# Score groups and late products with v on one ring of two PSUM tiles, block products on two bank pairs, and a new list of work

## The chip, the cores and the metric

The kernel runs on one core of one Trainium2 chip. The metric is device time in microseconds (us), from the start of the program to its end. TensorE (PE in the profile) multiplies matrices into PSUM, which has eight banks of 128 x 512 fp32 values; VectorE (DVE), ScalarE (ACT) and GpSimd (POOL) do the rest, and SyncE (SP) starts the transfers. PE's weight loads are listed apart, as PEld.

## What is computed

Attention with a mask by blocks of 64 rows, and behind it a two-layer feed-forward block with a squared ReLU. Batch 8, 8 heads, 576 rows, head size 64; 512 features, 2048 hidden.

```python
def _attn_ref(q, k, v):
    block = 64
    scale = 1.0 / np.sqrt(D)
    scores = scale * np.matmul(q, k.transpose(0, 1, 3, 2))
    mask = block_i >= block_j
    scores = np.where(mask, scores, -1000000000.0)
    scores = scores - np.max(scores, axis=-1, keepdims=True)
    attn = np.exp(scores)
    attn = attn / (np.sum(attn, axis=-1, keepdims=True) + 1e-09)
    return np.matmul(attn, v).astype(np.float32)
...
def _moe_ref(x, w_in, w_out):
    h = x @ w_in
    r = np.maximum(h, 0.0)
    g = r * r
    return (g @ w_out).astype(np.float32)
```

## The kernel before

**Tiling.** A pass is one pair of heads of one batch element. Passes 0 to 7 do the first three blocks of rows of batch elements 0 and 1, passes 8 to 15 the other six, and passes 16 to 39 all nine blocks of elements 2 to 7. A pass from 8 on has three score groups (`A20_0`, `A20_1`, `A20_2` in pass 20): PE writes the scores of two to four blocks of rows into one PSUM tile `side` of two banks, DVE takes each block's negative maximum (`B`, tile `nmx`), ACT the exponentials (`C`, tile `p`, sums `sm`), POOL and DVE the inverse of the sum (`S`, `R`), and ACT and DVE write the scaled rows as two fp16 parts (`H` and `L`, tile `p_rows`). A transfer turns them (`T`, `p_turned`), PE multiplies them with v (`G`, PSUM tile `px`), and `X` moves the result to SBUF.

**Chunks.** Twelve chunks of 384 tokens go through the feed-forward block, in the order 0, 1, 2, 4, 3, 5, 7, 6, 8, 10, 9, 11. The first three are plain: `ph` is one product with the first weights for 128 hidden features, `pos`, `sqr`, `top`, `rem` make its square into two fp16 parts (`hidden`). From chunk 4 on the first layer is a seven-product block scheme: for each of four groups of a chunk, PE runs p1, p2, p6, p5, p7, p4, p3 (`p14_0` is p1 of chunk 4, group 0). p1, p6, p7 and p4 add up in one bank, X; p2, then p5 and p3, use another, B. Between them ACT or DVE copies X (`c11` after p1, `c12` after p6, `c22` after p7, `c21` after p4) and DVE adds B to those copies (`a11` after p2, `a22` after p5, `a12` after p3). A product may start when the copy of what it overwrites or adds to is done. The scheme needs weights that are combined once on DVE, POOL and ACT (`t0_0` to `t3_17`; `p14_0` needs `t0_17`, the last of group 0's). `po` is the second layer: 16 steps of three products for each of three blocks of tokens, with the result scaled (`ob`) and stored (`out`).

**Order.** `ORDER` is a list of all pieces of work by name, with the engine where there is a choice (`:D`, `:A`, `:P` for DVE, ACT, POOL). `Plan.run` makes them in that order, and `Lines` ties each instruction to the one before it on its engine. So every engine works through its own part of the list, in order, and an instruction that waits holds up all that stands behind it on that engine. The list alone sets the order; the costs and ranks in `plan_all` are not used by it. How pieces of different engines stand to each other in the list says nothing of time.

**PSUM.** Banks are taken in turn from rings, and a piece that takes one waits until the pieces that read its last content are done. Up to pass 13 there are two `side` tiles, two `pair` banks (transposes, `ph`, `po`) and two banks `x` (transposes, `px`, sums for the norm, weight maxima). From pass 14 (`ALONE`) on all score groups use `side0` alone. The three banks thus given up (`side1` has two, `pair1` one) become a ring `group` of three for the block products, and `pair0` serves `po`. Two functions carry this: `side_of`, and `bank_of`, which closes the early pool:

```python
        if t["i"] >= ALONE:
            return 0
...
            homes[ring] = [ps_g.tile([P, 512], F32, name=f"group{n}") for n in range(3)]
```

## Time and profile before

| | |
|---|---|
| median of three runs | 963.83 us (962.95 to 963.94) |
| profiled execution | 963.4 us, of which the span is 961.6 us |
| PE busy, PE weight loads | 936.5 us, 602.6 us |
| DVE, ACT, POOL busy | 764.7, 638.6, 267.9 us |
| mean granted clock of PE | 0.995 of 2.4 GHz |
| by line of the chain that ended last | PE 81%, DVE 10%, ACT 3% |

The span is the profiled stretch of the execution; the other 1.8 us lie around it. A busy PE is a PE whose matmuls overlap without a gap in the records; the ends of matmuls are modelled, so a short wait can lie inside busy time. All instructions have line 331, since a helper records them: they are told apart by the names of their tiles.

### The profile page before, as it was taken

What the parts mean: (1) busy time and instruction counts of PE and PEld (TensorE: products, weight loads), DVE (VectorE), ACT (ScalarE), POOL (GpSimd) and SP (SyncE); (2) the same over time, 40 slices, a digit from 0 to 9 for tenths busy, and PEclk for the clock granted to TensorE, in tenths of its full rate; (3) what the DMA queues carried; (4) which work ended last, traced back from release to release, by engine and by line L of the source; (5) the groups of instructions that cost most, each with busy time, mean ns of one, the idle gap of its engine ahead of it and who ended that gap; (6) DMA issues with size and microseconds to landing.
All of it is one profiled execution on the core that took longest, in us unless ns stands there. A gap on an engine that the chain in (4) does not pass through costs nothing.

```text
span 961.6 us, 21188 instructions
## 1 busy us (share of the span) xinstructions
PE 936.5 (97%) x8145; PEld 602.6 (63%) x8145; DVE 764.7 (80%) x1703; ACT 638.6 (66%) x1585; POOL 267.9 (28%) x371
## 2 busy tenths in 40 slices
PE   8899899999998999999999999999999999999998
PEld 5455444545554784785676675686675675596675
DVE  6999997789899997899879788698879777656331
ACT  6999986765895786885475576678657555365330
POOL 4586401222255541224032032031112012011110
PEclk9999999999999999999999999999999999999999
DMA  9915477656855318435665346564473354400001
GB/s 358 399 63 186 153 163 164 139 135 136 188 115 121 83 51 190 104 63 118 124 155 123 78 107 112 119 150 94 86 176 84 74 117 81 91 13 12 12 1 45
DMA packets 221650, 114.93 MB, mean 120 GB/s; under 512 B 195290, under 2 KB 203756, under 8 KB 221548
## 3 DMA queue, kind: packets, MB, share of 16 engines
q1 hardware_dynamic: 221548, 113.57, 48.5%
q8 instruction: 64, 1.05, 0.4%
q14 instruction: 38, 0.31, 0.1%
HBM read 58.21 MB, written 9.46 MB: 70 GB/s over the span
## 4 chain that ended last, share of the span: by engine, by line
PE 81%; DVE 10%; ACT 3%; POOL 2%; issue 2%; DMA 2%; SPq 0%; DVEq 0%; ACTq 0%; POOLq 0%
PE pair L331 40%; PE group L331 24%; PE side L331 8%; PE px L331 6%; DVE nmx L331 2%; DVE p_rows L331 2%; PE po L331 2%; DVE w L331 2%; DMA w<-in_w_in 1%; POOL w L331 1%; DVE xt_all L331 1%; DVE stw L331 1%; DMA vraw<-in_v 1%; ACT p L331 1%; DVE x L331 1%
## 5 line engine op out<-in xcount | busy, mean ns | idle before, releaser
L331 PE MATMUL pair<-w,hidden 128*128 128x512 f16 (+1 forms) x1680 | 382.1, 376 | 1.0 <-DVE ob L331 0.9
L331 PEld LDWEIGHTS <-hidden 128*128 128x128 f16 x1776 | 168.5, 98 | 179.0 <-issue 11.7
L331 PEld LDWEIGHTS <-w 128*128 128x128 f16 x2304 | 200.4, 98 | 56.9 <-issue 10.3
L331 ACT ACTIVATE p<-side,nmx 128x576 f32<-128x576 f32 (+8 forms) x264 | 140.1, 541 | 94.3 <-DVE nmx L331 45.6
L331 POOL TENSOR_TENSOR hidden<-r,hidden 128x384 f16<-128x384 f32 x103 | 104.0, 1020 | 219.7 <-ACT hidden L331 204.6
L331 PE MATMUL group<-xt_all,w 128*128 128x192 f16 x1728 | 161.8, 247 | 0.8 <-DVE xt_all L331 0.5
L331 DVE SCALAR_TENSOR_TENSOR p_rows<-p,rs,p_rows 128x64 f16<-128x64 f32 (+7 forms) x264 | 147.2, 578 | 11.0 <-ACT p_rows L331 8.8
L331 DVE TENSOR_REDUCE nmx<-side 128x1 f32<-128x192 f32 (+8 forms) x288 | 123.4, 481 | 27.2 <-PE side L331 26.4
L331 POOL TENSOR_SCALAR sm<-sm 128x2 f32<-128x2 f32 (+2 forms) x104 | 34.5, 332 | 333.2 <-ACT p L331 316.0
L331 PE MATMUL group<-xt_all,turned_w 128*128 128x192 f16 x1296 | 122.8, 246 | 0.0
L331 PEld LDWEIGHTS <-turned_w 128*128 128x128 f16 x1296 | 108.1, 98 | 14.2 <-issue 4.9
L331 ACT ACTIVATE p_rows<-p,rs 128x64 f16<-128x64 f32 (+11 forms) x173 | 90.3, 554 | 31.8 <-DVE rs L331 21.2
L331 ACT ACTIVATE r<-group,rescale 128x384 f32<-128x384 f32 x111 | 63.7, 579 | 69.2 <-PE group L331 61.5
L331 ACT ACTIVATE r<-r 128x384 f32<-128x384 f32 x177 | 90.9, 523 | 20.0 <-DVE r L331 17.7
L331 ACT CAST hidden<-r 128x384 f16<-128x384 f32 x172 | 84.7, 507 | 28.8 <-DVE r L331 19.1
L331 DVE SCALAR_TENSOR_TENSOR r<-group,rescale,r 128x384 f32<-128x384 f32 x108 | 65.9, 613 | 45.8 <-PE group L331 32.5
L331 PE MATMUL side<-qk 64*64 64x512 f32 (+2 forms) x480 | 97.0, 498 | 3.5 <-ACT p L331 3.4
L331 PE MATMUL pair<-xt_all,w 128*128 128x384 f16 x576 | 98.9, 326 | 1.1 <-DVE xt_all L331 0.7
L331 PE MATMUL side<-ks,qk 64*64 64x192 f32 (+4 forms) x576 | 91.9, 424 | 0.0
L331 PE MATMUL px<-p_turned,v 128*64 128x384 f16 (+5 forms) x1168 | 66.8, 269 | 0.3 <-ACT p_turned L331 0.3
L331 PEld LDWEIGHTS <-v 128*64 128x64 f16 x1128 | 48.5, 110 | 21.5 <-issue 11.3
L331 DVE TENSOR_TENSOR hidden<-r,hidden 128x384 f16<-128x384 f32 x89 | 51.3, 579 | 7.5 <-ACT hidden L331 7.1
(154 smaller groups left out, 1060.3 us busy)
## 6 DMA issues: line engine op xcount, KB each, us to landing
qk<-in_qk SPq DMA_DIRECT2D x32, 576.0 KB
ks<-in_ks SPq DMA_DIRECT2D x32, 320.0 KB
vraw<-in_vm SPq DMA_DIRECT2D x30, 256.0 KB
w<-in_w_out SPq DMA_DIRECT2D x10, 512.0 KB
out<-ob SPq DMA_DIRECT2D x17, 256.0 KB
w<-in_w_in SPq DMA_DIRECT2D x8, 512.0 KB
out<-ob SPq DMA_DIRECT2D x26, 128.0 KB
hidden<-in_w_in SPq DMA_DIRECT2D x6, 512.0 KB
```

The lines of the kernel that those rows point to most:

```text
L331: i = make(*a, **k)
```

## The change

All eight banks are given out once, for the whole program: two `side` tiles of two banks, two banks `pair`, two banks `single`.

- Score groups take the two `side` tiles in turn to the end (ring `s`). The products with v of passes 12 to 39 take one tile of the same ring, one half for each of the two parts.
- X of group g is `pair0` for even g and `pair1` for odd g, and B is the other one. So p1 of a group goes into the bank that p3 of the group before has filled, and waits for that group's `a12`; p2 waits for that group's `c21`.
- `single` serves as ring `x` early on; later `single0` is ring `y` (norm sums, v's maxima, two of the last four outputs) and `single1` is `po`.
- `ORDER` is another list. The rest of the code, the sizes and the number of matmuls stay.

```diff
-p0 A0 B0 C0 p1 A1 A2 B1 S0 R0 C1 r0 max0_0 prelu0_0 B2 D0:P S1 R1 C2 r1 prelu0_1 bits0_0 A3 p2 D1:P E0 F0:A A4 r2 B3 C3 E1 max0_1 A5 bits0_1 S2
+p0 p1 r0 r1 p2 A0 r2 r3 A1 r4 B0 C0 p3 B1 r5 C1 S0 A2 R0 r6 D0:D r7 prelu0_0 max0_0 bits0_0 A3 r8 B2 r9 S1 E0 prelu0_1 bits0_1 keys8 R1 max0_1 C2
...
-    ps_x = ctx.enter_context(tc.tile_pool(name="ps_x", bufs=2, space=PSUM))
-    sides = [ps_b.tile([P, 1024], F32, name="side0")]
-    pairs = [ps_b.tile([P, 512], F32, name="pair0")]
-    early = ExitStack()
-    ps_e = early.enter_context(tc.tile_pool(name="ps_e", bufs=1, space=PSUM))
-    sides.append(ps_e.tile([P, 1024], F32, name="side1"))
-    pairs.append(ps_e.tile([P, 512], F32, name="pair1"))
-    homes = {"mm": pairs, "po": pairs[:1]}
-    turns_of = dict(mm=0, po=0, g=0)
+    bank = lambda name, n: ps_b.tile([P, 512 * n], F32, name=name)
+    pairs, singles = ([bank(f"{name}{n}", 1) for n in range(2)] for name in ("pair", "single"))
+    homes = {"s": [bank(f"side{n}", 2) for n in range(2)], "mm": pairs, "x": singles, "y": singles[:1], "po": singles[1:]}
+    turns_of = {ring: 0 for ring in homes}
...
-        if ring not in homes:
-            early.close()
-            ps_g = ctx.enter_context(tc.tile_pool(name="ps_g", bufs=1, space=PSUM))
-            homes[ring] = [ps_g.tile([P, 512], F32, name=f"group{n}") for n in range(3)]
...
-            ps = box["ps"] = sides[side_of(t, group)]
+            ps = box["ps"] = bank_of("s")
...
-        full = ps_x.tile([P, 512], F32, tag="x", name=f"px_{u}_{g}")
+        if t["whole"]:
+            full = bank_of("x")
+        else:
+            if "home" not in t:
+                t["home"] = bank_of("s")
+            full = t["home"][:, 512 * (1 - g) :]
...
-            box[name] = bank_of("g")[:, :CH]
+            box[name] = pairs[(g + (name == "B")) % 2][:, :CH]
...
-                    ("p1", lows("01") + weights + ([f"p2{ck}_{g - 1}"] if g else []), ("g",)),
-                    ("p2", [f"p1{k}"], ("g",)),
+                    ("p1", lows("01") + weights + ([f"p2{ck}_{g - 1}"] if g else []), (f"g{g % 2}",)),
+                    ("p2", [f"p1{k}"], (f"g{1 - g % 2}",)),
```

Two places in the order, with the numbers of the tiles. The first is DVE's part around the first product of the block scheme, `p14_0`. `nmx_3_1_0_8` holds the maxima of `A21_2` and `nmx_3_2_0_4` those of `A22_0`; `t0`, `t2`, `t3` are combined weights; the row `w1<-t0` is `t0_17`. Before:

```order
L331 SCALAR_TENSOR_TENSOR p_rows_93<-p32_3_1_0_7_3604,rs_3_1_0_7_3718,p_rows_93 128x128
L331 TENSOR_SCALAR m_3_2_0_3734<-pm_3_2_0_3646 128x2
L331 TENSOR_TENSOR turned_w_105<-t2_AluOpType.subtract_0_3639,turned_w_105 128x2x256
L331 SCALAR_TENSOR_TENSOR p_rows_93<-p32_3_1_0_7_3604,rs_3_1_0_7_3718,p_rows_93 128x384
L331 SCALAR_TENSOR_TENSOR p_rows_93<-p32_3_1_0_7_3604,rs_3_1_0_7_3718,p_rows_93 128x512
L331 TENSOR_REDUCE nmx_3_1_0_8_3748<-side0_75 128x1 x2
L331 TENSOR_SCALAR nmx_3_1_0_8_3748<-nmx_3_1_0_8_3748 128x2
L331 TENSOR_TENSOR xt_all_106<-x32_97,xt_all_106 128x768
L331 TENSOR_TENSOR w1_107<-t0_AluOpType.subtract_1_3752,w1_107 128x2x256
L331 TENSOR_TENSOR xt_all_106<-s2_2_1_3721,xt_all_106 128x384
L331 TENSOR_REDUCE nmx_3_2_0_4_3883<-side0_75 128x1 x4
```

After:

```order
L331 TENSOR_TENSOR w1_103<-t0_AluOpType.subtract_1_3526,w1_103 128x2x256
L331 TENSOR_TENSOR s2_2_1_3563<-s1_2_1_3552,x32_93 128x384
L331 TENSOR_TENSOR xt_all_102<-s1_2_1_3552,xt_all_102 128x384
L331 TENSOR_TENSOR t3_AluOpType.subtract_0_3618<-w1_103 128x512
L331 SCALAR_TENSOR_TENSOR p_rows_89<-p32_3_0_0_8_3528,rs_3_0_0_8_3543,p_rows_89 128x576
L331 TENSOR_TENSOR t3_AluOpType.subtract_0_3618<-t3_AluOpType.subtract_0_3618,w1_103 128x512 x2
L331 TENSOR_TENSOR xt_all_102<-s2_2_1_3563,xt_all_102 128x384
L331 SCALAR_TENSOR_TENSOR p_rows_89<-p32_3_0_0_8_3528,rs_3_0_0_8_3543,p_rows_89 128x448
L331 TENSOR_TENSOR turned_w_101<-t3_AluOpType.subtract_0_3618,turned_w_101 128x2x256
L331 TENSOR_REDUCE nmx_3_2_0_4_3674<-side0_76 128x1 x4
L331 TENSOR_SCALAR nmx_3_2_0_4_3674<-nmx_3_2_0_4_3674 128x4
L331 TENSOR_REDUCE nmx_3_1_0_8_3687<-side1_77 128x1 x2
```

Before, `A21_2` and `A22_0` both stand in `side0`; now they stand in `side1` and `side0`, and the two maxima follow each other. `t0_17` stood behind the maxima of `A21_2` and stands ahead of them now. Up to and with it DVE's part of the list has 629 instructions before and 601 now. PE's part up to `p14_0` has 396 matmuls of `po` before and 336 now, and `G20`'s 42 matmuls no longer stand there; the rest is the same work but for two small matmuls of v's maxima.

The second place is ACT's part in chunk 3, the second chunk of the block scheme, from the first copies of group 0 to those of group 1 (`r12_3_1` is the copy `c12` of chunk 3, group 1). Before:

```order
L331 ACTIVATE r12_3_0_5005<-group2_3839,rescale_112 128x384
L331 ACTIVATE p32_4_0_0_8_5008,sm_4_0_0_8_5009<-side0_75,nmx_4_0_0_8_4956 128x576
L331 ACTIVATE p32_4_0_0_8_5008,sm_4_0_0_8_5009<-side0_75,nmx_4_0_0_8_4956 128x448
L331 CAST xt_all_106<-x32_97 128x2x96
L331 ACTIVATE r11_3_1_5026<-group1_3838,rescale_112 128x384
L331 ACTIVATE r22_3_0_5058<-group2_3839,rescale_112 128x384
L331 ACTIVATE p_rows_93<-p32_4_1_0_4_4903,rs_4_1_0_4_4954 128x128
L331 ACTIVATE p_rows_93<-p32_4_1_0_4_4903,rs_4_1_0_4_4954 128x64
L331 CAST hidden_109<-r11_3_0_4989 128x2x192
L331 ACTIVATE r12_3_1_5095<-group1_3838,rescale_112 128x384
L331 ACTIVATE r21_3_0_5097<-group2_3839,rescale_112 128x384
```

After:

```order
L331 ACTIVATE ob_4_2_5059<-single1_75,uv_4_4519 128x512
L331 ACTIVATE ob_4_2_5059<-ob_4_2_5059,uv_4_4519 128x512
L331 ACTIVATE r21_3_0_5089<-pair0_72,rescale_108 128x384
L331 ACTIVATE r12_3_0_4994<-r12_3_0_4994 128x384 x2
L331 CAST hidden_105<-r12_3_0_4994 128x2x192
L331 ACTIVATE r21_3_0_5089<-r21_3_0_5089 128x384
L331 CAST hidden_105<-r22_3_0_5029 128x2x192
L331 ACTIVATE r12_3_1_5141<-pair1_73,rescale_108 128x384
L331 CAST hidden_105<-r21_3_0_5089 128x2x192
```

Before, copies of group 1 (bank `group1`) stand between those of group 0 (`group2`): two groups are open at once. Now the last copy of group 0, `r21_3_0`, stands ahead of group 1's `r12_3_1`. Over the nine chunks p1 of the next group stands ahead of the last product of a group 25 times of 27 before, and once now.

## Rows read from the trace of the kernel before

**Rows 1.** the page: span and part 1 (busy us, share, instructions).

```profile
span 961.6 us, 21188 instructions
...
PE 936.5 (97%) x8145; PEld 602.6 (63%) x8145; DVE 764.7 (80%) x1703; ACT 638.6 (66%) x1585; POOL 267.9 (28%) x371
```

**Rows 2.** busy time by stretch: us, PE, PEld, DVE, ACT, POOL, clock, DMA.

```profile
0.00:120.00 120.00, 103.82 (x799) 61.47 (x800) 108.75 (x256) 108.56 (x289) 70.79 (x104) 0.97 0.63 232
120.00:300.00 180.00, 180.00 (x1315) 92.90 (x1314) 157.58 (x359) 130.76 (x327) 48.10 (x67) 1.00 0.66 147
300.00:322.00 22.00, 18.88 (x171) 12.28 (x173) 19.26 (x32) 11.83 (x28) 11.94 (x12) 0.92 0.45 82
322.00:820.00 498.00, 496.85 (x4740) 338.44 (x4733) 416.78 (x943) 333.03 (x834) 117.03 (x168) 1.00 0.50 110
820.00:830.00 10.00, 9.10 (x48) 4.08 (x43) 6.36 (x15) 3.40 (x8) 0.19 (x1) 1.00 1.00 202
830.00:955.00 125.00, 125.00 (x1064) 91.16 (x1063) 55.42 (x102) 50.98 (x100) 19.90 (x21) 1.00 0.05 13
955.00:961.60 6.60, 2.85 (x27) 2.32 (x24) 0.54 (x1) 0.00 (x0) 0.00 (x0) 0.98 0.30 79
```

**Rows 3.** timeline of PE, 303 to 314: start, length, work [idle, releaser].

```profile
304.09 2.26 PE L331 MATMUL px<-p_turned,v 128*64 128x192 f16 x42
306.40 2.10 PE L331 MATMUL pair<-w,hidden 128*128 128x512 f16 x9
311.58 0.49 PE L331 MATMUL side<-qk 64*64 64x320 f32 x2 [3.07 <-ACT p L331]
...
313.52 3.44 PE L331 MATMUL group<-xt_all,w 128*128 128x192 f16 x24
```

**Rows 4.** timeline of DVE and ACT in the same stretch.

```profile
305.50 3.08 DVE L331 SCALAR_TENSOR_TENSOR p_rows<-p,rs,p_rows 128x384 f16<-128x384 f32 x2
...
308.50 1.27 DVE L331 TENSOR_REDUCE nmx<-side 128x1 f32<-128x576 f32 x2
...
310.08 0.74 ACT L331 ACTIVATE p<-side,nmx 128x576 f32<-128x576 f32 x1 [2.97 <-DVE nmx L331]
...
312.06 0.69 DVE L331 TENSOR_TENSOR w<-_AluOpType.subtract,w 128x512 f16<-128x512 f32 x1 [1.22 <-ACT w L331]
```

**Rows 5.** busy time and granted clock just after 312, and around 826.

```profile
312.00:315.00 3.00, 3.00 (x29) 2.04 (x20) 2.94 (x6) 1.17 (x3) 2.84 (x3) 0.63 0.54 100
315.00:318.00 3.00, 3.00 (x30) 2.83 (x28) 2.97 (x7) 2.10 (x8) 1.35 (x2) 0.80 0.00 0
824.00:827.00 3.00, 2.10 (x11) 0.87 (x10) 2.02 (x4) 0.37 (x2) 0.00 (x0) 1.00 1.12 204
```

**Rows 6.** waits of PE: who for whom, us in total, times, longest.

```profile
PE pair L331 <- DVE ob L331: 0.9, 1, 0.9
...
PE group L331 <- DVE xt_all L331: 0.5, 1, 0.5
...
PE group L331 <- DVE r L331: 0.2, 1, 0.2
```

**Rows 7.** timeline of PE and ACT, 393 to 398: one group's first products.

```profile
393.80 2.14 PE L331 MATMUL group<-xt_all,w 128*128 128x192 f16 x24
...
394.99 0.58 ACT L331 ACTIVATE r<-group,rescale 128x384 f32<-128x384 f32 x1 [1.87 <-PE group L331]
...
395.78 1.15 PE L331 MATMUL group<-xt_all,turned_w 128*128 128x192 f16 x12
...
396.77 1.15 PE L331 MATMUL group<-xt_all,w 128*128 128x192 f16 x12
```

**Rows 8.** timeline of DVE and ACT: maxima and exponentials of a score group.

```profile
314.11 1.21 DVE L331 TENSOR_REDUCE nmx<-side 128x1 f32<-128x320 f32 x4
...
318.04 0.21 ACT L331 ACTIVATION_READ_ACCUMULATOR p<-side,nmx 128x1 f32 x1
```

**Rows 9.** timeline of PE, 129 to 143: one unbroken run of output steps.

```profile
129.54 13.77 PE L331 MATMUL pair<-w,hidden 128*128 128x512 f16 x63
```

More of the change, by code (lines that the diff above doesn't have):

```diff
@@ L173 @@
-t2_11 l42_1 H21_1_0:A h52_1:A L21_1_2 fc22 fd22 t2_12:D L21_1_1 po2_1_15 A21_2 L21_1_0 B21_2 t0_13:P ob2_1:A G20 t0_14:P po2_2_0 po2_2_1 po2_2_2 C21_2
-out2_1 A22_0 l012_1 po2_2_3 t0_15:P t0_16 h232_1:A t0_17:D p14_0 s42_1:P h62_1:A l52_1 p24_0 T21_0_1 S21_2 c114_0:A p64_0 B22_0 po2_2_4 t3_0:P l232_1
-a114_0 T21_0_0 t3_1:P C22_0 c124_0:A R21_2 t3_2:P H21_2_1:A S22_0 t2_13:D p54_0 t1_13:D t3_3 R22_0 p74_0 t3_4:P H22_0_1:D t1_14:D po2_2_5 t3_5:D
-t1_15:D c224_0:A t1_16 H21_2_0:A H22_0_3:A l62_1 a224_0 t3_6:P t1_17:D t2_14:P po2_2_6 H22_0_0:A sq114_0:A A22_1 L21_2_1 T21_1_0 t2_15:P H22_0_2:A
@@ new lines @@
+po2_0_11 po2_0_12 po2_0_13 po2_0_14 po2_0_15 s42_1:P A21_2 ob2_0:A t3_0:D A22_0 L20_2_0 h232_1:A out2_0 p14_0 t3_1:D h62_1:A h52_1:A p24_0 t3_2:D
+c114_0:A l52_1 t3_3 po2_1_0 L20_2_1 fv22 po2_1_1 T20_1_1 t3_4:D B22_0 po2_1_2 t3_5:P po2_1_3 B21_2 po2_1_4 t3_6:P po2_1_5 po2_1_6 t2_13:D t3_7 po2_1_7
+C21_2 t3_8:D t2_14:P po2_1_8 po2_1_9 R21_1 po2_1_10 l232_1 H21_1_1:A S21_2 t2_15:P H21_1_2:A H21_1_0:A p64_0 a114_0 t3_9:P R21_2 L21_1_2 po2_1_11
+c124_0:A L21_1_1 po2_1_12 H21_2_1:A t3_10:P fv23 A22_1 L21_1_0 po2_1_13 B22_1 C22_0 po2_1_14 po2_1_15 p54_0 t3_11 l62_1 S22_0 ob2_1:D sq114_0:A p74_0
@@ new lines @@
+po7_0_2 h64_0:A l64_0 po7_0_3 B30_2 X28_0:A po7_0_4 A31_0 C30_2 po7_0_5 B31_0 po7_0_6 S30_2 G29 R30_2 a127_3 C31_0 sq127_3:D H30_2_0:D L30_2_0 S31_0
+A31_1 T30_0_1 X29_0:A rem217_2:P h54_0:A X29_1:D top127_3 vh30:A B31_1 rem127_3:P T30_0_0 H30_2_1:A po7_0_7 po7_0_8 po7_0_9 L30_2_1 po7_0_10 T30_1_0
+top227_2 rem227_2:P po7_0_11 R31_0 vl30 C31_1 po7_0_12 sq217_3:D po7_0_13 T30_1_1 po7_0_14 S31_1 H31_0_2:D H31_0_1:D H31_0_0:A H31_0_3:D po7_0_15
+L31_0_1 L31_0_3 H31_0_4:A L31_0_2 A31_2 ob7_0:A L31_0_0 R31_1 A32_0 L31_0_4 B31_2 top217_3 out7_0 po7_1_0 H31_1_1:A rem217_3:P vals32 po7_1_1 B32_0
@@ L709, in turned @@
         def turned():
-            pm = box["pm"] = ps_x.tile([P, 512], F32, tag="x", name=f"pm_{u}")
+            pm = box["pm"] = bank_of("x" if pair[0]["i"] == WHOLE else "y")
             nc.tensor.transpose(pm[:2, :P], box["st"], ident)
@@ L784, in scores @@
                 nc.tensor.matmul(ps[D * h : D * h + D, o], q[rs], keys[rs, k], start=True, stop=True)
-    def side_of(t, group):
-        if t["i"] >= ALONE:
-            return 0
-        n = [j for g, _, _ in t["groups"] for j, _ in g[:1]].index(group[0][0])
-        return (t["i"] * len(t["groups"]) + n) % 2
     def rows(t, group):
@@ L911, in turn @@
                 if t["first"]:
-                    pt = ps_x.tile([P, 512], F32, tag="x", name=f"pt_{k}")
+                    pt = bank_of("x")
                 else:
@@ L1361, in products @@
                 ring = out_ring(ck, n)
-                bank = ps_x.tile([P, 512], F32, tag="x", name=f"po_{ck}_{n}") if ring == "x" else bank_of(ring)
-                box["po"] = bank[:, :w]
+                box["po"] = bank_of(ring)[:, :w]
             for i, (z, k) in enumerate(((0, 0), (0, 1), (1, 0))):
@@ L1534, in row_steps @@
             largest = 880 if short else 1.07 * w + 100 * n + 90
-            ring = f"s{side_of(t, group)}"
+            ring = "s"
             add(f"A{k}", "PE", score, after + ([f"A{i - 1}_{n}" for n in range(3)] if NT * NHP < i < 16 else []), rank + (3 if short else 0), start, (ring,), frees=frees)
@@ L1618, in norm @@
             step = lambda n: lambda *q: box["s"][n](*q)
-            add(f"hb{k}", "DVE", 680 if big == 1 else 950, frees, rank, start, ("hb",), frees=[(f"nq{k}", "x")])
+            add(f"hb{k}", "DVE", 680 if big == 1 else 950, frees, rank, start, ("hb",), frees=[(f"nq{k}", x_of_norm(b, g))])
             add(f"xm{k}", "DVE", 160 + 0.985 * size, [f"hb{k}"], rank, step("scaled"), frees=[(f"hb{k}", "hb")])
```

445 lines of the change are left out of this document (223 added, 222 removed).

## The prediction

> **What bounds the kernel now.** I read the page's first part, then busy time by stretch, then the waits of PE, then the timeline around the largest of them. The page says PE: it is busy for 936.5 of 961.6 us [rows 1], so 25.1 us of gaps are all that a new order could remove if the matmuls stay, and they do. The table by stretch shows where the gaps lie. The first 120 us hold 16.2 (120 less 103.82), 120 to 300 none, 300 to 322 hold 3.1, 322 to 820 hold 1.15, 820 to 830 hold 0.9, 830 to 955 none, and the last 6.6 us hold 3.75 [rows 2]. Within the gapless stretches nothing is hidden that is worth a term: 63 output matmuls in a row take 13.77 us [rows 9], 0.2186 us each at most, where 512 columns at 2.4 GHz are 0.213.
>
> So there are three places. The start is not PE's: DVE is busy for 108.75 and ACT for 108.56 of the first 120 us [rows 2], and PE waits for what they make. The end is the last output's scaling and store. What is left is the wait at 308.5 and a few small ones.
>
> At 308.5 PE has run out of work that stands ahead of `A22_0`, and `A22_0` waits 3.07 us for ACT's exponentials of `A21_2`, since both stand in `side0` [rows 3]. Those were late because DVE came to the maxima only at 308.50, after two `p_rows` instructions that took 3.08 us [rows 4]. The clock then falls: 0.63 granted in 312 to 315 and 0.80 in 315 to 318 [rows 5], which is 3 x 0.37 + 3 x 0.20 = 1.7 us of work at 2.4 GHz, lost while PE is busy. The place costs 3.1 + 1.7 = 4.8 us in all.
>
> **The change part by part.** The sum is made against the profiled execution, 963.4 us, which is 0.4 below the median of 963.83; the 0.4 is added at the end.
>
> *A second tile for scores.* `A22_0` no longer needs the exponentials of `A21_2`, so the 4.8 us go. Behind them in PE's new list stand p1 and p2 of chunk 4's first group and 16 steps of `po`, at most 0.656 us each (three of the matmuls of rows 9), so the next score group has over 12 us of PE work in front of it. What is late next is `p14_0`, below.
>
> *Late products with v in the score ring.* This is a new wait: a product takes a score tile, and a score group may wait for a product. At one place of the new list the work between is too short: `A31_1` takes the tile of `A31_0`, with two steps of `po` (1.3 us) and `G29` between them (2.26 us for 42 such matmuls [rows 3]), 3.6 us. The maxima and exponentials of such a group took from 314.11 to 318.25 [rows 8], 4.1 us. That is 0.6 us of wait, on the path. At the other places the cover is of the order of a chain's length or longer, and I put nothing there.
>
> *Two banks in place of three for the block products.* Nothing is added to the work, but groups no longer overlap, and with that the work between a product and the one that needs its copy gets shorter. A product is 0.99 us (from 395.78 to 396.77 [rows 7]). The copy of X started at 394.99, 0.2 us after p1's twelve matmuls at 0.0825 us had been streamed (393.80 + 0.99 = 394.79), and took 0.58. So a hand-over needs 0.8 us, and one product of other work covers it with 0.2 to spare. I counted the hand-overs in both lists (p6 after p1, p5 after p2, p7 after p6, p4 after p7, p3 after p5, p2 after the p4 of the group before, and, where the bank is now the same, p1 after that group's p3). With at most one product's length of other work between they are 23 of 207 before and 63 of 234 now. What the 23 cost shows in the waits of PE: group products waited 0.2 us in all for DVE's `r` [rows 6], 0.009 each, and waits too short for the records may lie beside it. At that price 63 cost 0.5 us. The upper end is that half of them find a 0.58 us instruction queued in front of the copy, 0.29 us for each of the 40 more, 11.6 us. Below nothing it can't be, since these waits can at best be absent. I take 0.5, since the 23 are the same kind of place on the same engines, and keep 11.6 for a rival.
>
> *The rest of the new list.* The waits of 0.9 us for `ob` at 826 and 0.5 us for `xt_all` [rows 6] belong to places that have been rewritten: minus 1.4. Waits of their kind will stand elsewhere, as nothing in the change is aimed at them; I take the same 1.4 back. Bounds are 0 and 6, the latter for four more of the longest.
>
> *The start.* Up to the first product of chunk 1, DVE's part of the list has 235 instructions before and 238 now, ACT's 209 and 211, POOL's 92 and 89. Three DVE instructions at 764.7/1703 = 0.449 us [rows 1] are 1.3 us, ACT and POOL nearly cancel. DVE idles for 11.25 of the first 120 us [rows 2], so the order can also gain. I take 0, between minus 4 (a third of DVE's idle time) and plus 1.3. The end keeps its form, a half-width block, its scaling and its store: 0.
>
> Sum: 963.4 - 4.8 - 1.4 + 0.6 + 0.5 + 1.4 = 959.7, and with the 0.4 that the median stands higher 960.1; I say 960.0.
>
> **The rivals.**
>
> *The wait moves to `p14_0`.* This one can end on the slow side. `p14_0` stood behind the wait and started at 313.52 [rows 3]; `t0_17`, which it needs, ended at 312.06 + 0.69 = 312.75 [rows 4]. So the old wait hid another that was almost as long. In the new list PE has 60 `po` matmuls (20 steps, 13.1 us) and `G20` (2.3 us) less in front of it, and without the old wait it gets there 15.4 + 3.1 + 0.4 us (the slow clock's part before it) sooner, at 294.6. DVE has 28 instructions less up to `t0_17`, 12.6 us at 0.449: done at 300.2, if it idles as much before that as it did. PE would wait 5.6 us, and the clock fall once more: 7.3 us, 967.4 in all, slower. For it speaks that DVE is behind all through the first 120 us. Against it: DVE idled for 22.4 us between 120 and 300 [rows 2], and a quarter of that less, 5.6 us, removes the wait. It decides from about 6: if wait and lost clock together exceed that, the change is slower. *Half of it*, 2.8 us of wait and 1.7 of clock, gives 964.6, no difference.
>
> *The hand-overs wait.* 40 more short hand-overs at 0.29 us: 960.1 + 11.6 = 971.7. For it: on an in-order engine that is 80% busy [rows 1] a copy seldom finds its engine free. Against it: the 23 places with the same cover lost 0.2 us [rows 6].
>
> *The clock falls at the hand-overs.* The drop after the 3.07 us wait cost 1.7 us [rows 3, 5]. If every third of the 36 groups ended in a wait that brings one, 12 x 1.7 = 20 us, 980. The 0.9 us gap at 826 left the granted clock at 1.00 [rows 5], which speaks against it. The Trainium skill describes this course (TensorE: Matmul & The Clock Gate, section "A second HAM failure mode: psum-queue depth-cycling"): cycling through PSUM banks leaves small gaps between groups of matmuls, and the clock swings between its two levels. The trace of before, with 23 short hand-overs and one drop after 120 us, does not show it.
>
> *The start gets shorter.* The gap of DVE there by 4 us: 956.
>
> *It does not do what it says.* If the second tile changed nothing because DVE, not the tile, is what the score groups wait for, the 3.1 us come back at the next group. That is the half case above, by another way; it is counted there.
>
> **How the numbers follow.** A measurement of this kernel can tell 0.2% from no change, 1.9 us: faster is below 961.9, slower above 965.8. The forecast gets 0.47 (0.44 of it faster, 0.03 within), the shorter start 0.05 (faster). Half of the moved wait gets 0.20 (0.19 within, 0.01 slower), the whole of it 0.14, the hand-overs 0.10 and the clock 0.04, all slower. Together: faster 0.49, the same 0.22, slower 0.29. The range reaches from 954.5, below the shorter start, to 970, which takes in the moved wait and hand-overs at 0.25 us. The forecast's own range is 957 to 963. Outside stay most of the hand-over case, the clock and a little on the low side, under 0.2.
>
> **What would show it right or wrong.** In the profile of after: PE's waits should have no 3 us entry of `side` for ACT's `p`, and the granted clock no drop between 290 and 330. If the wait moved, a row of PE's first `pair` product with `xt_all` near 295 has an idle time of 2 us or more before it, ended by DVE's `w` or `xt_all`, with a drop of the clock behind it. If the hand-overs wait, the waits of `pair` products for `r` sum to over 5 us, or PE's steps of 0.99 us stretch without a gap in the records. The start is judged by PE's busy time in the first 120 us, 103.8 now. The forecast is wrong if PE's gaps after 120 us sum to more than 8 us (8.9 now, with the end), or if the start loses more than 2 us.

## The result, and the profile after

The changed kernel takes 953.89 us (953.63 to 954.66), the kernel before beside it 963.88 (962.95 to 964.57): a ratio of 0.9898, with a 95% interval of 0.9881 to 0.9915. It is 10.0 us faster, where 3.8 were forecast, and lies 0.6 us below the range. The profiled execution took 953.77 us, of which the span is 952.0; it answers to [rows 1]:

```profile
span 952.0 us, 21220 instructions
...
PE 929.8 (98%) x8145; PEld 603.9 (63%) x8145; DVE 753.0 (79%) x1698; ACT 656.6 (69%) x1620; POOL 238.6 (25%) x353
```

The span is 9.6 us shorter. Of that, 6.7 us are busy time of PE (936.5 to 929.8) with the same 8145 records, and only 2.9 us are gaps (25.1 to 22.2). So most of the gain lies where the records show no gap at all; 1.7 of the 6.7 are the slow clock of [rows 5], which the records count as busy time, and some 5 are left to be explained. By stretch, with the columns of [rows 2]:

```profile
0.00:120.00 120.00, 103.64 (x810) 61.03 (x810) 110.32 (x260) 110.83 (x297) 62.09 (x101) 1.00 0.70 243
120.00:300.00 180.00, 179.87 (x1348) 95.41 (x1347) 161.51 (x358) 142.63 (x351) 54.14 (x72) 1.00 0.63 142
300.00:322.00 22.00, 20.43 (x200) 14.19 (x199) 20.37 (x37) 17.20 (x44) 11.69 (x13) 1.00 0.46 88
322.00:820.00 498.00, 497.19 (x4735) 340.21 (x4733) 399.26 (x936) 338.74 (x841) 89.33 (x146) 1.00 0.52 112
820.00:830.00 10.00, 10.00 (x75) 6.52 (x74) 6.52 (x17) 4.30 (x9) 0.59 (x1) 1.00 0.15 28
830.00:945.00 115.00, 114.92 (x955) 83.47 (x953) 54.43 (x94) 42.90 (x82) 20.73 (x22) 1.00 0.05 13
945.00:952.00 7.00, 3.74 (x35) 3.11 (x32) 0.54 (x1) 0.00 (x0) 0.00 (x0) 0.97 0.24 80
```

The gap of 3.1 us at 300 to 322 has become 1.6, that of 0.9 at 820 to 830 is gone, and 120 to 300 holds 1348 matmul records where it held 1315, with no gap before and almost none now. The granted clock of this execution is 1.00 in every stretch but the last 7 us (0.97); its three other executions had 0.996 to 0.998 on average.

Behind 120 us PE has two waits left that the records show (engine, tile and line, what for: us in all, times, longest us):

```profile
PE side L331 <- ACT p L331: 1.5, 1, 1.5
PE side L331 <- ACT x L331: 0.7, 1, 0.7
```

The first stands at the place of [rows 3], but in front of another piece: `A22_0` finds its tile free, and now `G20`, the product with v of pass 20, waits for the tile of `A22_0`. PE (start, length, work, [idle, releaser]):

```profile
307.47 1.15 PE L331 MATMUL pair<-xt_all,turned_w 128*128 128x192 f16 x12
310.08 2.26 PE L331 MATMUL side<-p_turned,v 128*64 128x192 f16 x42 [1.45 <-ACT p L331]
312.26 0.82 PE L331 MATMUL single<-w,hidden 128*128 128x512 f16 x3
```

ACT's exponentials of `A22_0` write into a buffer that DVE is still reading for `p_rows`, and POOL works beside them:

```profile
308.25 0.53 ACT L331 ACTIVATE p<-side,nmx 128x320 f32<-128x320 f32 x1 [2.45 <-DVE p_rows L331]
...
304.31 3.91 DVE L331 SCALAR_TENSOR_TENSOR p_rows<-p,rs,p_rows 128x128 f16<-128x128 f32 x3
308.14 1.34 DVE L331 TENSOR_REDUCE nmx<-side 128x1 f32<-128x512 f32 x3
...
303.92 1.16 POOL L331 TENSOR_TENSOR _AluOpType.subtract<-_AluOpType.subtract,w 128x512 f32<-128x512 f32 x1
305.03 1.21 POOL L331 TENSOR_TENSOR _AluOpType.subtract<-w,_AluOpType.subtract 128x512 f32<-128x512 f16 x1
306.32 1.35 POOL L331 TENSOR_TENSOR _AluOpType.subtract<-_AluOpType.subtract,w 128x512 f32<-128x512 f32 x1
```

It is the place of [rows 4] once more: long `p_rows` instructions on DVE, and behind them what frees a tile.

**Where the busy time went.** A score group that stands alone takes 0.92 or 1.03 us from its first matmul to the next step's, and the step ahead of it is longer too. Before, PE around 338 and 347 us:

```profile
338.01 0.65 PE L331 MATMUL side<-qk 64*64 64x512 f32 x2
...
339.04 1.16 PE L331 MATMUL group<-xt_all,turned_w 128*128 128x192 f16 x12
...
345.98 1.15 PE L331 MATMUL group<-xt_all,turned_w 128*128 128x192 f16 x12
346.97 1.15 PE L331 MATMUL group<-xt_all,w 128*128 128x192 f16 x12
348.06 0.49 PE L331 MATMUL side<-qk 64*64 64x320 f32 x2
...
348.98 1.16 PE L331 MATMUL group<-xt_all,turned_w 128*128 128x192 f16 x12
```

One group takes 339.04 - 338.01 = 1.03, the other 348.98 - 348.06 = 0.92. The product ahead of the second takes 348.06 - 346.97 = 1.09, the one ahead of that 0.99. In the changed kernel groups stand in pairs, since two tiles allow it:

```profile
348.25 4.04 PE L331 MATMUL single<-w,hidden 128*128 128x512 f16 x18
352.22 0.49 PE L331 MATMUL side<-qk 64*64 64x320 f32 x2
...
352.93 0.60 PE L331 MATMUL side<-qk 64*64 64x512 f32 x2
...
354.01 2.77 PE L331 MATMUL single<-w,hidden 128*128 128x512 f16 x12
```

The pair takes 354.01 - 352.22 = 1.79 where two alone take 1.95, and the price at the entrance is paid once. Over the whole trace behind 120 us there are 24 pairs now and none before. 22 of them are 0.162 to 0.164 us shorter than two lone groups, one 0.148 and one 0.080, which makes 3.8 us in all. The entrance costs 0.094 us whenever a score group or a product with v follows a step that uses the whole array; a score group next to a product with v pays it once. Before, the list has 80 such entrances behind 120 us, now 73.

So each step can be charged: the time from its first matmul to the next step's, less the shortest time of its form (lone groups for score groups). Worked out from all PE records, us:

```
                     start   pairs  late by   short  end    sum
                    (119 us)        > 0.25
before               26.3     0.0     7.8      8.6   3.6   46.3
after                25.0    -3.6     3.8      8.1   3.1   36.4
difference           -1.3    -3.6    -4.0     -0.5  -0.5   -9.9
```

"Pairs" holds all score groups: the 24 pairs give 3.8, one lone group that is late takes 0.2 back. "Late" are the other steps that lose over 0.25 us. At the place near 308 us these are 4.9 us before and 1.9 after, elsewhere 2.9 and 1.9. "Short" holds the entrances. The parts add up to 9.9 where the span is 9.6 us shorter, so they are good to a few tenths. The start is the weakest: executions that have the same first 120 us in their order differ there by up to 1.9 us (five traces with the start of before, at the product `G13`), and each row of the table is one execution.

### The profile page after: what moved, and what is told of

Read it like the earlier page. It is cut to its first block, busy times and chain, and to the rows that moved or that the text cites. A ratio compares the mean times of both kernels' runs of the same rounds, so it can differ in the third digit from the quotient of the medians.

```text
span 952.0 us, 21220 instructions
## 1 busy us (share of the span) xinstructions
PE 929.8 (98%) x8145; PEld 603.9 (63%) x8145; DVE 753.0 (79%) x1698; ACT 656.6 (69%) x1620; POOL 238.6 (25%) x353
## 4 chain that ended last, share of the span: by engine, by line
PE 78%; DVE 10%; DMA 5%; ACT 5%; issue 2%; POOL 0%; SPq 0%; ACTq 0%; DVEq 0%; POOLq 0%
PE pair L331 37%; PE single L331 29%; PE side L331 12%; DVE nmx L331 2%; DVE p_rows L331 2%; DVE w L331 2%; DMA p_turned<-p_rows 2%; ACT p L331 1%; DMA turned_w<-in_w_in 1%; DMA vraw<-in_vt 1%; DMA w<-in_w_out 1%; ACT r L331 1%; ACT p_rows L331 1%; DVE xt_all L331 1%; DVE _AluOpType.subtract L331 0%
## 5 line engine op out<-in xcount | busy, mean ns | idle before, releaser
L331 PE MATMUL single<-w,hidden 128*128 128x512 f16 (+1 forms) x1488 | 335.0, 372 | 0.1
L331 PE MATMUL pair<-xt_all,w 128*128 128x192 f16 (+1 forms) x2304 | 260.2, 266 | 1.1 <-DVE xt_all L331 0.7
L331 DVE SCALAR_TENSOR_TENSOR p_rows<-p,rs,p_rows 128x128 f16<-128x128 f32 (+7 forms) x264 | 139.4, 554 | 9.4 <-ACT p_rows L331 7.8
L331 DVE TENSOR_REDUCE nmx<-side 128x1 f32<-128x64 f32 (+8 forms) x288 | 123.3, 480 | 15.0 <-PE side L331 14.5
L331 ACT ACTIVATE r<-pair,rescale 128x384 f32<-128x384 f32 x139 | 80.8, 584 | 68.5 <-PE pair L331 64.7
L331 PE MATMUL pair<-xt_all,turned_w 128*128 128x192 f16 x1296 | 124.7, 246 | 0.1
L331 DVE SCALAR_TENSOR_TENSOR r<-pair,rescale,r 128x384 f32<-128x384 f32 x108 | 66.3, 614 | 57.5 <-PE pair L331 41.3
L331 PE MATMUL side<-qk 64*64 64x512 f32 (+2 forms) x480 | 90.6, 488 | 4.2 <-ACT p L331 3.4
L331 PE MATMUL pair<-w,hidden 128*128 128x512 f16 x288 | 64.6, 379 | 0.0
L331 PE MATMUL side<-p_turned,v 128*64 128x384 f16 (+3 forms) x1128 | 62.0, 265 | 1.5 <-ACT p L331 1.5
```

The lines of the kernel that those rows point to most:

```text
L331: i = make(*a, **k)
```

## The experiments

The pieces of the order are quoted as they stand on one engine. Ratios are against the kernel before as it was measured beside each run; differences from the changed kernel are against its 953.89 us. The kernel before took 963.0 to 963.9 each time.

### Pairs taken apart, second group later

TensorE's order, one of 24 places:

```diff
-po4_0_7 A23_0 A23_1 po4_0_8
+po4_0_7 A23_0 po4_0_8 A23_1
```

> The changed kernel with its 24 pairs of score groups that stand directly behind one another in TensorE's order taken apart: the second group of each pair goes behind the next step (one step of the second layer or one product), nothing else moves. Theory A, that a group which is followed by another saves 0.16 us because it shares the end of the first with the start of the second: 24 x 0.16 = 3.9 us slower than the changed kernel, 957.8 us, and in the trace 48 lone groups of 0.92 to 1.03 us. Rival B, that the shorter groups of the changed kernel's trace are only a shift of time into the next step: within 0.7 us of 953.9. A group that comes one step later could also make its maxima late and add a wait; that would show as an entry in PE's waits, and not as longer groups.

Measured: 961.26 us, ratio to before 0.9973 (0.9962 to 0.9984), 7.4 us slower than the changed kernel. The place that was quoted for the changed kernel, 352 to 354 us:

```profile
353.95 0.49 PE L328 MATMUL side<-qk 64*64 64x320 f32 x2
...
354.87 0.82 PE L328 MATMUL single<-w,hidden 128*128 128x512 f16 x3
355.62 0.65 PE L328 MATMUL side<-qk 64*64 64x512 f32 x2
...
356.64 0.61 PE L328 MATMUL single<-w,hidden 128*128 128x512 f16 x2
```

The groups are back at 0.92 and 1.02, and the step of `po` between them takes 0.75 where others take 0.65. Rival B falls. The price was above the 3.9 expected, since the second entrance of each pair was left out of it: by the table's working the score groups lose 3.6 us, the short losses 2.6 (24 x 0.094 = 2.3), the late steps 0.6.

### Pairs taken apart, first group earlier

```diff
-po4_0_15 A23_2 A24_0 po4_1_0
+A23_2 po4_0_15 A24_0 po4_1_0
```

> The changed kernel with 23 of its 24 pairs of score groups taken apart the other way: the first group of the pair goes one step earlier in TensorE's order, the second stays where it is, so that no maxima come later than in the changed kernel. With the second group moved one step later the kernel took 961.3 us: 3.9 us of that stand in longer score groups, the rest in waits of single products. Theory A, that being next to another group is worth 0.16 us: 23 x 0.162 = 3.7 us, 957.6, and fewer waits than with the later groups. Rival B, that the 7.4 us came from groups that were late: 953.9 to 955.

Measured: 959.35 us, ratio 0.9951 (0.9938 to 0.9965), 5.5 us slower than the changed kernel. 23 x (0.162 + 0.094) = 5.9. That the two ways of taking apart cost 7.4 and 5.5 bounds what lateness adds; the pair itself is worth about a quarter of a microsecond.

### More pairs

A21_1 behind the norm's sums to A20_2, A34_1 up to A34_0, A39_0 down to A39_1, and two groups two steps later:

```diff
-A24_2 po4_2_0 po4_2_1
+po4_2_0 po4_2_1 A24_2
```

> The changed kernel with three more pairs of score groups (A21_1 and A20_2, A34_0 and A34_1, A39_0 and A39_1 moved next to each other by one to eight steps) and two groups that waited, A24_2 and A33_0, two steps later on TensorE. By theory A three pairs are worth 0.5 us, and the two waits 0.3 and 0.9: 952.2. If the waits only move to the next group or product, 953.4; if an earlier group of a pair waits for its tile, over 954.

Measured: 956.76 us, ratio 0.9925 (0.9912 to 0.9937), 2.9 us slower than the changed kernel. The pairs gave what they promise (score groups 0.7 us less), but four new waits came: a norm's sum waits 1.0 us for DVE's squares, the second layer 0.9 for `ob`, a product 0.7 for its copy, and `G20` waits 2.4 in place of 1.5. A pair is worth having only where the order has room for it.

### Neighbours in the kernel before taken apart

26 places where a score group and a product with v are neighbours, such as

```diff
-A21_2 G20 po2_2_0
+A21_2 po2_2_0 G20
```

> The kernel before, with its banks, in which 26 times a score group and a product with v stand next to each other on TensorE (after the first 120 us); each of these is taken apart by one step of the second layer, of a product or of the first layer, nothing else moves. In the traces a step ahead of a score group or of a product with v takes 0.094 us longer than ahead of another step, and one of the two ahead of the other takes nothing extra. Theory A, that this is time and not only where the records put it: 26 x 0.094 = 2.4 us slower than before, 966.2, with no new entry in PE's waits. Rival B, that the extra 0.094 us is hidden work that some other step pays anyway: 963.8, within 0.7.

Measured: 970.24 us, ratio 1.0069 (1.0055 to 1.0082), 6.9 us slower. The short losses rise by 3.0 us, near the 2.4 expected. The late steps rise by 3.1, in several places: 1.1 ahead of a norm's sum at 291 us, which waits for DVE's squares, 0.9 at the place near 308, 0.5 at a product near 332 that waits for its copy, 0.4 near 477. At 308 `G20` no longer stands ahead of the second layer's step, and it is this step that waits now, longer than `A22_0` did:

```profile
PE pair L328 <- ACT ob L328: 3.7, 1, 3.7
```

So the entrance is time in the other kernel as well, though over half of what this run lost is not the entrance.

### One tile for the late score groups

From pass 14 on `side0` for score groups, `side1` for products; the list is otherwise the changed kernel's, with pieces put off to where their tile is free.

```diff
-            ps = box["ps"] = bank_of("s")
+            ps = box["ps"] = bank_of("s0" if t["i"] >= 14 else "s")
...
-                t["home"] = bank_of("s")
+                t["home"] = bank_of("s1")
```

> The changed kernel without the second tile for late score groups: from pass 14 on they all use side0, and the late products with v use side1 alone. The list is the changed kernel's, with each piece that would now take a full tile moved to where the tile is free (14 score groups go 3 to 23 steps later on TensorE, the pieces that need them follow). Theory A, that the tile is worth the pairs (none are left, 3.9 us) and the place near 308 us (3 us): about 961, with the wait for ACT's p back near 308. Rival B, the prediction's view that only the place near 308 counts: 957. Rival C: under 955, the tile is worth nothing once the list is good.

Measured: 1069.96 us, ratio 1.1098 (1.1083 to 1.1113). No theory had that.

```profile
PE side L328 <- ACT p L328: 76.8, 41, 4.8
```

41 score groups wait 1.9 us each for the exponentials of the group before. The run says nothing about the price of a tile under a list made for one; it says that the new list needs the second tile at 41 of its 78 score groups from pass 14 on, not at 308 us alone.

### The clock held at the large wait

```diff
+        def fill_group():
+            spin(bank_of("g"), 13)
+            turns_of["g"] = 0
...
+        plan.ahead = {"A22_0": fill_group}
...
+            if name in self.ahead:
+                self.ahead[name]()
```

> The kernel before, with 13 matmuls of 512 columns whose results nobody reads put on PE directly ahead of the score group that waits 3.07 us at 308.5 us; they take 13 x 0.213 = 2.8 us of the wait. What is waited for stays. Theory A, that the drop of the granted clock behind the wait costs 1.7 us by itself: 962.2, with a clock of 1.00 from 308 to 320 us. Rival B, that the slow clock only covers a wait that the next product has anyway: 963.9. The wait itself is still paid, so it can't be under 962.

Measured: 963.75 us against 963.44, ratio 1.0003 (0.9994 to 1.0012). In PE's timeline the 13 matmuls fill the wait, and the next one takes over:

```profile
309.51 2.97 PE L331 MATMUL group<-ones_bf 128*128 128x512 bf16 x13
312.74 0.49 PE L331 MATMUL side<-qk 64*64 64x320 f32 x2 [0.26 <-ACT p L331]
...
319.07 1.15 PE L331 MATMUL group<-xt_all,w 128*128 128x192 f16 x12 [0.96 <-DVE r L331]
```

The clock is held (the columns of the table by stretch; 0.63 in [rows 5]):

```profile
312.00:315.00 3.00, 2.74 (x31) 1.61 (x29) 1.78 (x3) 2.34 (x6) 2.68 (x3) 1.00 0.99 180
```

The two traces put a number on the place itself: PE stands 1.17 us later than in the kernel before at `A21_2`, ahead of the place, and 1.18 us later at `A23_1`, behind it. With the clock held or not, the place costs the same. With it held, the next product waits 0.96 us for its copy `r` (the second row): the slow clock had covered waits of this kind. The 1.7 us were no term.

### The clock held in the start

Its edit is the same, with `plan.ahead` for `E8_0_2` (9 matmuls) and `E10_0_1` (7) into `pair0`.

> The kernel before with 9 and 7 matmuls of 512 columns whose results nobody reads put on PE inside its two waits of the start (2.15 us ahead of the transposes at 38.2 us, 1.8 us ahead of those at 75.7 us), which are the waits behind which the granted clock fell. What is waited for stays. Theory A, that each of the two drops costs the work lost in it (3.4 us in all): 960.2. Theory B, that PE's speed does not matter there, since DVE and ACT set the pace (executions of the kernel before with a mean clock of 0.990 took 961.7 to 962.7 us and those with 0.995 took 961.4 to 961.9): 963.4 to 963.9, with fewer drops in the profile.

Measured: 966.21 us, ratio 1.0025 (1.0014 to 1.0037), slower. The first filling came too late: PE had been idle for most of the time from 34 us on, and the nine matmuls themselves ran at half the clock, so that they outlasted the wait by 1.3 us, in PE's timeline:

```profile
35.94 3.75 PE L331 MATMUL pair<-ones_bf 128*128 128x512 bf16 x9
```

By stretch the second drop, at 77 us, is gone:

```profile
36.00:39.00 3.00, 3.00 (x9) 1.04 (x8) 2.97 (x7) 2.32 (x8) 1.89 (x5) 0.50 1.09 360
...
78.00:81.00 3.00, 3.00 (x28) 1.66 (x27) 2.96 (x10) 3.00 (x8) 2.75 (x4) 1.00 0.76 226
```

A gain from the second is not seen, but the run does not price the first. All 80 executions of the kernel before that were timed beside these runs tell more. The 18 with a mean clock of 0.990 or 0.991 took 964.2 us on average, the 28 with 0.995 or 0.996 took 963.2. The lost work differs by some 4.4 us, the time by 1.0. This is what goes together, not a cause shown: no run sets the clock of the start apart from the rest.

### New start with the old rest, old start with the new rest

The list of one kernel up to `ph1_0`, the first product of chunk 1 (about 115 us), and behind it the other's.

> The kernel before, with its banks, and of the new list only the part up to the first product of chunk 1 (about the first 115 us); the rest stands in the old order. Theory A, that the start has a share of its own (the two drops of the granted clock at 39.7 and 77.3 us cost 3.4 us of work, and PE's order runs 1.4 us earlier by 121 us): 1.4 to 3.4 us faster than before, 960.5 to 962.5, with no drop of the clock ahead of 120 us. Rival B, that what the start gains is waited for again at the large wait near 308 us, which ends with DVE and not with PE: 963.9, and the wait there longer by what was gained.

Measured: 963.52 us, ratio 1.0002 (0.9994 to 1.0011). At the seam, where the two lists meet, PE loses what the start gained (by 128 us it stands 1.4 us later than in the kernel before), and the wait near 308 is 3.1 us as before. Such a difference lies within the 1.9 us by which executions with the same start differ.

> The converse: the changed kernel, with its banks and its list, but with the old order up to the first product of chunk 1. Theory A: the changed kernel plus what the start is worth, 953.9 + 1.4 to 3.4 = 955.3 to 957.3, with the two drops of the clock at about 40 and 77 us back and none later. Rival B, that the start is worth nothing: 953.9. If the start and the rest do not add up (a DVE that is behind its old place makes the new order wait near 300 us), over 958.

Measured: 956.74 us, ratio 0.9928 (0.9915 to 0.9942), 2.9 us slower than the changed kernel. In the trace PE is 3.3 us behind the changed kernel as early as `A14_0` (123 us) and 3.4 at the end, so all of the difference stands in the start and at the seam. The two do not add up: the start is worth nothing in front of the old rest and 2.9 us in front of the new one, of which the seam and the scatter may be a part. The new rest with its banks is worth 6.7 us by itself.

### Maxima first in the kernel before

DVE's order:

```diff
-L21_1_1 L21_1_0 B21_2
+B21_2 L21_1_1 L21_1_0
```

> The kernel before with one place of its list changed: DVE takes the maxima of A21_2 ahead of the two instructions on p_rows (3.08 us) that stood in front of them, so that the score group A22_0 finds its tile free without a second tile. Theory A, the term of the prediction (wait and clock there are worth 4.8 us): 958.7 to 959. Theory B, that DVE bounds this stretch: the work on DVE up to the first products stays, only its idle 1.22 us ahead of t0_17 can go, and the wait moves to p14_0 or to the product that needs a114_0: 962.2. Rival C, nothing at all: 963.4.

Measured: 961.15 us, ratio 0.9970 (0.9959 to 0.9982): 2.75 us faster (1.7 to 4.0), between A and B. In the trace PE is 0.7 us ahead of the kernel before when it comes to the place and 2.7 ahead behind it, so the place itself gave 2.0. That is two thirds of the 3.0 us that the changed kernel gained there, with one tile and three names in another order. Something else changed as well, on DVE:

```profile
304.84 1.27 DVE L328 TENSOR_REDUCE nmx<-side 128x1 f32<-128x576 f32 x2
...
307.11 1.27 DVE L328 SCALAR_TENSOR_TENSOR p_rows<-p,rs,p_rows 128x384 f16<-128x384 f32 x2
```

The two `p_rows` instructions take 1.27 us, where the same two took 3.08 [rows 4]. In the kernel before POOL combined weights beside them:

```profile
303.84 1.20 POOL L331 TENSOR_TENSOR _AluOpType.subtract<-w 128x512 f32<-128x512 f16 x1 [2.65 <-DVE xt_all L331]
305.11 2.92 POOL L331 TENSOR_TENSOR _AluOpType.subtract<-_AluOpType.subtract,w 128x512 f32<-128x512 f32 x2
```

That opened the last question: is DVE late there because of POOL?

### Three combinations of weights on DVE, in either kernel

In the kernel before, behind the maxima of `A21_2`; in the changed kernel `t2_15`, `t3_9`, `t3_10` behind those of `A22_1`:

```diff
-t0_13:P t0_14:P t0_15:P
+t0_13:D t0_14:D t0_15:D
```

> The kernel before with three combinations of weights (t0_13, t0_14, t0_15) on DVE instead of POOL, behind the maxima of A21_2. In its trace they run on POOL from 303.8 to 308.0 us, while DVE's two instructions on p_rows ahead of the maxima take 1.51 and 1.64 us. Theory A: the two take 0.61 and 0.74 us, as they do where POOL rests, the maxima come 1.8 us sooner, and the wait of A22_0 falls from 3.1 to 1.3 us; since the three now stand ahead of t0_17 on DVE, p14_0 gains only 0.9 us: 962.6. Prediction's view, that a wait so much shorter gives back its length and the clock: 960.2. Rival B, nothing, since DVE has the same amount to do: 963.6.

Measured: 962.04 us against 963.86, ratio 0.9978 (0.9969 to 0.9987), 1.8 us faster. DVE and PE:

```profile
305.39 1.27 DVE L328 SCALAR_TENSOR_TENSOR p_rows<-p,rs,p_rows 128x384 f16<-128x384 f32 x2
...
309.66 0.49 PE L328 MATMUL side<-qk 64*64 64x320 f32 x2 [0.48 <-ACT p L328]
```

The wait fell from 3.1 to 0.5 us. The theory's limit at `p14_0` did not hold: `p14_0` starts at 311.24 and `t0_17` ends at 311.58, so the one does not wait for the other.

> The changed kernel with three combinations of weights (t2_15, t3_9, t3_10) on DVE instead of POOL, behind the maxima of A22_1 in DVE's list. In the changed kernel's trace they run on POOL from 303.9 to 307.7 us, while DVE's three instructions on p_rows take 0.92, 1.51 and 1.64 us; the forms of 384 and 512 columns take 0.68 and 0.81 on average over the kernel before. Theory A, that POOL's work beside them stretches them and that this is what the place near 308 waits for: the three take 2.0 us or less, the exponentials that G20's tile needs come 2 us sooner, G20 waits no more, 1.0 to 1.5 us faster than the changed kernel, 952.4 to 952.9. Rival B, that DVE's later work (three instructions of 0.69 us more) makes another product wait as long: 953.9.

Measured: 953.34 us, ratio to before 0.9892 (0.9878 to 0.9905), 0.55 us below the changed kernel, which is within the scatter. The mechanism is plain all the same:

```profile
304.40 1.52 DVE L328 SCALAR_TENSOR_TENSOR p_rows<-p,rs,p_rows 128x128 f16<-128x128 f32 x3
...
308.64 2.26 PE L328 MATMUL side<-p_turned,v 128*64 128x192 f16 x42
310.82 0.82 PE L328 MATMUL single<-w,hidden 128*128 128x512 f16 x3
312.62 1.15 PE L328 MATMUL pair<-xt_all,w 128*128 128x192 f16 x12 [0.98 <-DVE r L328]
```

The three `p_rows` take 1.5 us and not 3.9, `G20` waits for nothing, and 1.0 of its 1.45 us comes back ahead of `p34_0`. POOL's three instructions (3.7 us of POOL) made DVE's `p_rows` 2.4 us longer by running beside them; done on DVE itself they take 2.05 us. The time alone does not tell the theory from its rival; the rows do.

### What the edits add up to

> The changed kernel with two score groups moved: A39_0 one step later, next to A39_1 (a 25th pair, 0.23 us by the two kernels with the pairs taken apart), and A33_0 two steps of the second layer later, away from G31, behind which it waited (0.7 us idle, 1.6 us with what the two steps are longer by). Theory A: 0.2 to 1.8 us faster, 952.1 to 953.7. Rival B, that a list in which every place has been chosen loses somewhere else what it gains here, as the five moves of the kernel with more pairs did: 954.5 or more.

Measured: 953.23 us, ratio to before 0.9893 (0.9876 to 0.9910): 0.7 us below the changed kernel, within the scatter.

> The changed kernel with the two score groups moved (A39_0 next to A39_1, A33_0 two steps later) and the three combinations of weights on DVE behind the maxima of A22_1. If the two edits add up, 0.7 us (measured for the first, within the scatter) and 1.0 to 1.5 us: 951.7 to 952.3, faster than both kernels. If they do not, 953.2.

Measured: 952.77 us, ratio to before 0.9890 (0.9875 to 0.9905), 1.1 us below the changed kernel. Its late steps are 2.0 us in all (3.8 in the changed kernel). Executions lie at 952.2 to 953.8, those of the changed kernel at 953.6 to 954.7: probably the fastest of all, but by less than the interval.

> The kernel with both moves (two score groups moved, three combinations of weights on DVE behind the maxima of A22_1), and in it two further combinations, t3_12 and t3_13, behind a224_0 in DVE's list. With the two edits, PE's wait ahead of G20 is gone and the next product in line, p34_0, waits 0.98 us for a224_0, in front of which DVE has t3_12 and t3_13 (0.68 and 0.69 us). Theory A, that DVE's order is all that this wait hangs on: it goes, 951.8. Rival B, that the wait moves on once more, to a product that needs t3: 952.8.

Measured: 955.04 us, ratio 0.9919 (0.9906 to 0.9933), 2.3 slower than without the third move. The wait stays, and a second one joins it:

```profile
313.06 1.15 PE L328 MATMUL pair<-xt_all,w 128*128 128x192 f16 x12 [0.98 <-DVE r L328]
319.30 1.15 PE L328 MATMUL pair<-xt_all,w 128*128 128x192 f16 x12 [2.05 <-DVE r L328]
```

Rival B, and more than it said: what was put behind `a224_0` is now late for others. From A22_0 to G20 to p34_0 the wait has moved each time to the next piece that needs DVE; the place gets smaller, not empty.

## Why the prediction was wrong

The direction held, and so did what was said of the hand-overs; the time missed by 6.1 us. The largest single part is a term that the sum does not have. Forecast and measured by its own terms, us:

```
                                     forecast   measured
place near 308 (second score tile)     -4.8       -3.0
other late steps (ob, xt_all, A31_1,
  lone waits)                          +0.6       -1.0
hand-overs, entrances                  +0.5       -0.5
score groups in pairs                    -        -3.6
start                                   0         -1.3
end                                     0         -0.5
sum                                    -3.7       -9.9
```

- **The step that failed** is the sentence that within the gapless stretches nothing is hidden that is worth a term. It rested on 63 matmuls of one kind in a row [rows 9], and of these it is true. Nothing was asked about the places where the kind changes. The second tile was priced only by the one wait that it removes; that it lets score groups stand next to each other was in the new list to be read, 24 times, and has no wait to show for it. That is 3.6 of the 6.1 us that the forecast missed, and taking the pairs apart cost 7.4 and 5.5 us. The Trainium skill has the rule (TensorEngine Tiling (Array Packing), section "Key Properties"): a change of the tiling mode, as against a change of tile, drains TensorE. The rows agree in that a price stands where whole-array steps give way to parts of the array, 0.094 us each time; what it consists of no run shows. Between the two kinds of parts they differ from it: a product with v (128*64) next to a score group (64*64) pays nothing more, and here the measurement decides.
- **The place near 308** was 3.0 us, not 4.8. Two things were mis-sized. The clock's 1.7 us were counted as time because PE was busy while it was slow; with the clock held the kernel took the same time. And the wait was taken as gone, with its next victim sought at `p14_0` and `A31_1`. It came at `G20`, 1.45 us, by the mechanism that the prediction named for `A31_1`: a late product takes a score tile. Which product, and how long, it got wrong: `A31_1` does not wait at all. The 3.08 us of two `p_rows` instructions were read as DVE's work; without POOL beside them they take 1.27.
- **The moved wait** did not come. `p14_0` starts at 292.01 behind the pair A21_2, A22_0 without a gap (the prediction's estimate was 294.6). It could not have come there, since `p14_0` does not need `t0_17`, against what the prediction and the description of the kernel before say: it reads other weights than `t0_17` writes. In two runs with the new banks it starts while `t0_17`, the second of two such instructions on DVE, is still running (with the second groups moved later it starts at 292.93 and `t0_17` ends at 293.68; with more pairs, shown here, at 292.63 and 293.82):

```profile
291.73 2.09 DVE L328 TENSOR_TENSOR w<-_AluOpType.subtract,w 128x512 f16<-128x512 f32 x2
292.63 2.15 PE L328 MATMUL pair<-xt_all,w 128*128 128x192 f16 x24
```

  So nothing ties the row that starts at 313.52 before to the one that ends at 312.75, and the chances of 0.20 and 0.14 rested on a wait that these runs do not show. DVE was also earlier than reckoned: `t0_17` ended at 291.97 in the changed kernel, not at 300.2. DVE's idle time between 120 and 300 fell from 22.4 to 18.5 us [rows 2], not quite to the 16.8 that the rival asked for.
- **The hand-overs** were right. Products wait 0.2 us in all for a copy in the whole trace, in the start. Behind 120 us no product of the scheme behind another product or a `po` step loses more than 0.011 us. The short losses of products and steps beside them fell from 2.4 to 1.4 us, but nearly all of that are entrances, which fell with the neighbours. Both rivals on the hand-overs fell. So did the course that the Trainium skill describes (TensorE: Matmul & The Clock Gate, section "A second HAM failure mode: psum-queue depth-cycling"): block products cycle through two banks, and the clock stays at 1.00 in every stretch up to 945 us; in the last 7 us it is 0.97, with PE busy for 3.7 of them.
- **The start** was taken as 0 between minus 4 and plus 1.3. The trace says minus 1.3, the exchange of starts minus 2.9 or nothing. That is within the bounds, but a single execution can't tell minus 1.3 from nothing, as executions with the same start differ by up to 1.9 us. Whether the start is worth more in front of the new rest, and why, stays open.
- **The signs that it named** all came as for a right forecast: no 3 us entry for ACT's `p`, no drop of the clock between 290 and 330, PE's gaps behind 120 us 5.9 us (under 8), the start's busy time 103.6. All of them look at gaps. None could see a gain inside busy time, which is why the range ended too high: its low end came from a shorter start, and no case held steps that get shorter.

## What to carry to other kernels

Ask of every busy stretch what it would take as one kind of work in a row, and charge each change between matmuls on the whole array and on parts of it: here 0.094 us at the entrance and 0.16 us for a group that has no neighbour, 80 entrances behind 120 us in the kernel before. A wait that is taken away is worth its length only if the engine that released it is early for the next step; look for what that engine does in the microseconds before, and whether its instructions are longer there than elsewhere. A long instruction on DVE beside one on POOL need not be DVE's work: compare it with others of its own width over the kernel before building a term on it. And a wait that is feared for a piece needs that piece to read what the other engine makes: that two rows end and start next to each other does not show it.

## What the runs showed of the hardware

- **Two score groups in a row take less time than two apart.** 0.162 to 0.164 us less in 22 of 24 pairs, whichever of the two tiles comes first. That the matmuls of one group's end share the array with those of the next one's start is a guess; no run here takes that apart from other reasons.
- **DVE with two inputs in SBUF can take twice its time and more beside POOL; DVE on PSUM does not.** In the changed kernel 213 three-operand `p_rows` instructions have nothing on POOL beside them and 24 only a `TENSOR_SCALAR`: all are within 0.03 us of the median of their width. Of 27 with a `TENSOR_TENSOR` on POOL beside them 15 are longer, by 0.1 to 0.9 us. In the kernel before, 128x384 and 128x512 took 0.61 and 0.74 alone and 1.51 and 1.64 beside POOL. Of the changed kernel's 56 maxima of a tile `side`, which lies in PSUM, beside such a POOL instruction none was longer. The Trainium skill (SBUF — State Buffer, section "Who interferes with whom") says that a DVE instruction with two SBUF inputs contends with a GpSimd one that reads SBUF, for a shared pair of ports that the first one keeps for its whole instruction. The rows agree as to which instructions get longer; how the ports are held no run takes apart.
- **Most of the work lost to a slow clock was not time.** Two drops in the start of the kernel before,

```profile
39.00:42.00 3.00, 3.00 (x19) 1.67 (x17) 3.00 (x5) 2.78 (x7) 1.28 (x2) 0.62 1.03 415
78.00:81.00 3.00, 3.00 (x19) 1.55 (x18) 2.97 (x10) 2.95 (x7) 2.75 (x4) 0.56 0.70 204
```

  and one near 312 us [rows 5], each behind a wait of 1.8 us or more, cost PE some 1.7 us of work each. Holding the third gave nothing, and executions of the kernel before with some 4.4 us more of lost work were 1.0 us longer on average.
